# Eight tiles of split matmul input moved to eight different starts in SBUF

## The chip, the cores and the metric

The kernel runs on one core of one Trainium2 chip. The metric is the device time of one execution in microseconds; less is better. Inputs and outputs lie in HBM. SBUF, the on-chip memory that the engines read, has 128 partitions, and a tile takes the same range of bytes in each of them; where this document speaks of the place at which a tile begins, it means the byte within a partition, taken modulo 512.

## What is computed

Linear attention over 4 batches, 8 heads, 576 positions of 64 numbers each, followed by two MLPs over 2304 tokens of width 512 with 2048 hidden units. All is float32. Cut to what matters:

```
proj = x @ w_phi                      # 64 -> 128 features, for q and for k
proj -= max(abs(proj))                # per position
phi(x) = [exp(proj), exp(-proj)]      # 256 features
attn = phi(q) (phi(k)^T v) / (phi(q) sum(phi(k)) + 1e-6)
x = attn, heads side by side          # 2304 x 512
x = leaky_relu(x @ w1_in)  @ w1_out   # 512 -> 2048 -> 512
x = mish(x @ w2_in) @ w2_out
```

## The kernel before, in words

**Exact products out of rounded ones.** TensorE multiplies in the type float32r, which keeps fewer bits than float32. So each float32 operand x is split into a rounded part hi and a rest lo = x - hi, and a product is made of three matmuls into one PSUM bank: weights hi by input hi, weights hi by input lo, weights lo by input hi. `three` (lines 80 to 83) issues them on lines 81, 82 and 83. `split` (lines 76 to 78) makes the two parts: ScalarE rounds a copy into hi (line 77), VectorE subtracts it from the source into lo (line 78). In the names of the profile, a matmul `a<-wl,wh` writes a PSUM tile a, streams the tile wl (the moving operand) and holds 128 columns of wh (the stationary operand, brought in by a weight load, engine PEld, that has the line of its matmul).

**Attention** runs first, pair of heads by pair of heads (32 steps of `attention`, lines 435 to 485). `q_proj` and `k_proj` (lines 316 to 328 and 294 to 302) use `three` with moving operands of 256 or 320 columns; `kv` (line 345) and `nd` (line 373) use plain matmuls of 128 and 65 columns.

**The MLPs.** The tokens are cut into five blocks for each MLP, four of 512 tokens and one of 256, ten blocks in all, and worked through by `moe`. X (line 70) holds the activations transposed, in four chunks (kk = 0 to 3) of 128 features by 2304 tokens. For a block, `window` (lines 492 to 498) splits its four chunks into eight tiles: hi and lo for each kk. `emit_h` (lines 506 to 514) then makes the hidden units, 128 at a time: 16 groups (m), each with four chunks, each with `three`, where the tiles of the window are the moving operand (512 columns, or 256 in the short blocks) and slices of 128 columns of the split weights W are the stationary one. In the trace these are the matmuls `a<-wh,wh`, `a<-wl,wh` and `a<-wh,wl`: a weight tile and a window tile are both called wh or wl there. Window hi is the moving operand on lines 81 and 83, window lo on line 82. After the activation (`leaky`, lines 557 to 573, in the first MLP, `mish`, lines 575 to 622, in the second), whose result is again split into tiles gh and gl, `emit_o` (lines 516 to 533) makes the second product: `b<-gh,wh` and its like in the first MLP, where gh and gl stream, `b<-wh,gh` and its like in the second, where the weights stream.

**What sets the order.** The whole program is scheduled by hand: each engine runs its instructions in the order of the code. `moe` calls `emit_h` of the next groups before `emit_o` of an earlier one. When the last group of a block has been issued, `window` of the next block follows at once (lines 631 to 633). Its tiles are those that the old block's last matmuls still read, so ScalarE's copy for a chunk waits for the last matmul on that chunk, VectorE's subtraction waits for the copy, and TensorE meanwhile runs an `emit_o`.

**Where the tiles lie.** Pools are laid out one after another in the order of lines 62 to 68, slots inside a pool in the order in which their tags are first asked for. The pool of the window, winp (line 63), has four slots for each of its two tags, wh and wl (lines 495 and 496), of 512 numbers of 4 bytes, 2048 bytes each. In the program as built the eight slots begin at byte 53408 and follow each other every 2048 bytes, so all eight begin at 160 modulo 512. X begins at 128 modulo 512. The tiles that come after winp in the MLP stage, gh, gl and the weights W (whose slices of 128 columns are 512 bytes) among them, all begin at 160 modulo 512 too. In the attention stage the split inputs and weights of `q_proj` and `k_proj` begin at 0; `q_proj` streams from column 0 in its first two calls, from column 320 in its third (256 modulo 512) and from column 256 in its fourth (0 again). For `kv` the stationary operand begins at 64 and the moving one at 160 or 416; for `nd` the stationary operand begins at 128 or 384 and the moving one at 128. The last tile of the MLP stage ends at byte 227488 of a partition.

Of the kernel before, what the change touches and what calls it, by code (L numbers as in the profile page):

```python
# [12 lines left out]
F32R = mybir.dt.float32r  # L13
# [11 lines left out]
def attention_two_mlps_kernel(  # L25
# [17 lines left out]
    P = 128  # L43
    KD = DM // P
    M = DFF // P
    MAIN = 512
# [13 lines left out]
    I32 = mybir.dt.int32  # L60

    xp = tc.alloc_tile_pool(name="xp", bufs=1)
    winp = tc.alloc_tile_pool(name="winp", bufs=4)
    gp = tc.alloc_tile_pool(name="gp", bufs=2)
    wp0 = tc.alloc_tile_pool(name="wp0", bufs=1)
    ps = tc.alloc_tile_pool(name="ps", bufs=4, space=PSUM)
# [9 lines left out]
    def split(hi, lo, src):  # L76
        nc.scalar.activation(out=hi, in_=src, func=AF.Copy)
        nc.vector.tensor_tensor(out=lo, in0=src, in1=hi.bitcast(F32), op=ALU.subtract)
# [112 lines left out]
    with tc.manual_schedule():  # L191
# [297 lines left out]
        NB = len(blocks)  # L489
        win = {}  # L490

        def window(j, chunks=range(KD)):
            a, c0, n = blocks[j]
            for kk in chunks:
                hi = winp.tile([P, MAIN], F32R, tag="wh", name="wh")[:, 0:n]
                lo = winp.tile([P, MAIN], F32R, tag="wl", name="wl")[:, 0:n]
                split(hi, lo, X[:, kk, c0:c0 + n])
                win.setdefault(j, []).append((hi, lo))

# [128 lines left out]
        def moe(g):  # L628
            for x in [g, g + 1] if g == jump else [g + 1] if g > jump else [g]:
                if x < len(seq):  # L630
                    emit_h(seq[x])
                    if seq[x][1][-1] == M - 1 and seq[x][0] + 1 < NB:
                        window(seq[x][0] + 1)
# [42 lines left out]
        for n in range(PAIRS + 1):  # L676
            attention(n)
            if 0 <= n - PAIRS // 2 < KD:
                window(0, (n - PAIRS // 2,))
# [43 lines left out]
```

## Time and profile before

| | us |
|---|---|
| median of 3 runs | 1033.09 |
| lowest and highest of them | 1032.63, 1036.21 |
| the profiled execution, its own time | 1029.51 |
| its span in the trace | 1027.7 |

The profile shows that one execution. Engines: PE is TensorE's matmuls, PEld its weight loads (they run beside matmuls), DVE VectorE, ACT ScalarE, POOL GpSimd. A line of a timeline begins with the start and the duration in us. A matmul's duration in the trace includes the way through the array, so successive matmuls overlap in it: what one costs in a full stream is the distance from its start to the start of the next, called the step below. An instruction group in a fence of `--by-form` kind reads: line, engine, operation, out<-in, shapes, count | busy us, mean ns of one | idle time of the engine before them and what ended it.

### The profile page before, as it was taken

To read this page: it belongs to the slowest core of one execution; us is meant where nothing else is said; L and a number is where in the kernel's file an instruction comes from. 1 tells how busy PE (TensorE), PEld (TensorE's weight loads), DVE (VectorE), ACT (ScalarE), POOL (GpSimd) and SP (SyncE) were. 2 spreads that over 40 slices of the span, in tenths; PEclk is the share of its full clock that TensorE was granted. 3 is DMA by queue.
4 is the path that set the end of the run, shared out by engine and by line. 5 is a ranking of instruction groups with operands and counts; after the bars stand their busy time and mean duration, and the time that the engine had idled before them with its cause. 6 is when DMAs were issued, how large, how long until landed. Compare 5 with 4: busy or idle time off the path is not lost.

```text
span 1027.7 us, 14556 instructions
## 1 busy us (share of the span) xinstructions
PE 1001.1 (97%) x5544; PEld 871.2 (85%) x5544; DVE 753.2 (73%) x1389; ACT 501.3 (49%) x839; POOL 72.6 (7%) x38
## 2 busy tenths in 40 slices
PE   6999999999999999999999999999999999999998
PEld 5999988998888888998888888888888988888886
DVE  5888898876995666666533546978876888868976
ACT  4666666654554333343333445545544555545543
POOL 3322333220000000000000000000000000000000
PEclk9999999999999999999999999999999999999999
DMA  4333323313541344444311221000100100001001
GB/s 130 111 111 111 100 82 93 121 43 113 160 148 42 123 144 154 134 144 136 110 62 31 93 82 62 1 1 0 41 1 1 41 1 21 1 1 41 1 1 42
DMA packets 55494, 72.84 MB, mean 71 GB/s; under 512 B 10496, under 2 KB 39808, under 8 KB 55424
## 3 DMA queue, kind: packets, MB, share of 16 engines
q1 hardware_dynamic: 55264, 71.84, 21.6%
q8 instruction: 44, 0.72, 0.3%
q14 instruction: 26, 0.21, 0.1%
q10 hardware_dynamic: 160, 0.07, 0.0%
HBM read 57.48 MB, written 14.42 MB: 70 GB/s over the span
## 4 chain that ended last, share of the span: by engine, by line
PE 92%; DVE 5%; issue 1%; ACT 1%; POOL 0%; ACTq 0%; DVEq 0%; POOLq 0%
PE a L81 14%; PE a L82 14%; PE a L83 14%; PE b L82 13%; PE b L81 13%; PE b L83 13%; PE b L373 6%; PE b L345 4%; DVE qd L335 1%; PE a L266 1%; DVE kd L291 1%; DVE mx L290 1%; ACT kv L353 1%; PE b L395 1%; PE b L350 1%
## 5 line engine op out<-in xcount | busy, mean ns | idle before, releaser
L81 PE MATMUL a<-wh,wh 128*128 128x512 f32 (+1 forms) x640 | 235.6, 368 | 0.0
L82 PE MATMUL a<-wl,wh 128*128 128x512 f32 (+1 forms) x640 | 235.4, 368 | 0.0
L83 PE MATMUL a<-wh,wl 128*128 128x512 f32 (+1 forms) x640 | 235.4, 368 | 0.0
L81 PEld LDWEIGHTS a<-wh,wh 128*128 128x128 f32 x640 | 120.6, 188 | 20.2
L82 PEld LDWEIGHTS a<-wl,wh 128*128 128x128 f32 x640 | 120.7, 189 | 20.1
L83 PEld LDWEIGHTS a<-wh,wl 128*128 128x128 f32 x640 | 120.6, 188 | 20.0
L571 DVE TENSOR_TENSOR gl<-g,gh 128x512 fp32r<-128x512 f32 x72 | 49.9, 693 | 110.1 <-ACT gh L568 110.1
L82 PE MATMUL b<-gl,wh 128*128 128x512 f32 (+1 forms) x320 | 117.7, 368 | 0.0
L81 PE MATMUL b<-gh,wh 128*128 128x512 f32 (+1 forms) x320 | 117.7, 368 | 0.0
L83 PE MATMUL b<-gh,wl 128*128 128x512 f32 (+1 forms) x320 | 117.7, 368 | 0.0
L82 PE MATMUL b<-wl,gh 128*128 128x512 f32 x288 | 112.1, 389 | 0.0
L81 PE MATMUL b<-wh,gh 128*128 128x512 f32 x288 | 112.1, 389 | 0.0
L83 PE MATMUL b<-wh,gl 128*128 128x512 f32 x288 | 112.1, 389 | 0.0
L568 ACT ACTIVATE gh<-g 128x512 fp32r<-128x512 f32 x72 | 45.5, 632 | 115.9 <-PE b L83 109.4
L330 POOL PARTITION_ALL_REDUCE qm<-qd x32 | 71.9, 2249 | 140.7 <-DVE qd L335 122.1
L593 ACT ACTIVATE gh<-u 128x512 fp32r<-128x512 f32 x72 | 45.6, 633 | 70.6 <-PE b L82 63.9
L567 DVE TENSOR_TENSOR g<-g,a 128x512 f32<-128x512 f32 x72 | 49.4, 686 | 38.0 <-ACT g L564 35.2
L150 ACT ACTIVATE c<-c 128x512 f32<-128x512 f32 x64 | 40.3, 630 | 68.5 <-DVE c L147 68.3
L373 PE MATMUL b<-kv,qp 128*128 128x65 f32 x512 | 62.7, 276 | 7.5 <-ACT kv L353 7.5
L620 ACT ACTIVATE r<-e,two 128x512 f32<-128x512 f32 x72 | 51.7, 718 | 36.3 <-DVE e L605 36.3
L83 PEld LDWEIGHTS b<-gh,wl 128*128 128x128 f32 x320 | 60.3, 189 | 10.1
L81 PEld LDWEIGHTS b<-gh,wh 128*128 128x128 f32 x320 | 60.4, 189 | 10.0
(103 smaller groups left out, 1773.7 us busy)
## 6 DMA issues: line engine op xcount, KB each, us to landing
stage<-in_moe_w_in_dram SPq DMA_DIRECT2D x32, 512.0 KB, 3.6
stage<-in_moe_w_out_dram SPq DMA_DIRECT2D x32, 512.0 KB, 3.5
scr<-c SPq DMA_DIRECT2D x37, 256.0 KB, 2.0
wstage<-scr SPq DMA_DIRECT2D x32, 256.0 KB, 3.8
kn<-in_k_dram SPq DMA_DIRECT2D x16, 256.0 KB, 3.8
qn<-in_q_dram SPq DMA_DIRECT2D x16, 256.0 KB, 4.0
vmain<-in_v_dram SPq DMA_DIRECT2D x16, 256.0 KB, 3.2
out_dram<-X SPq DMA_DIRECT2D x16, 256.0 KB, 2.2
```

What stands on the lines that cost most here:

```text
L81: nc.tensor.matmul(out=o, lhsT=wh_, rhs=xh, start=start, stop=False)
L82: nc.tensor.matmul(out=o, lhsT=wh_, rhs=xl, start=False, stop=False)
L83: nc.tensor.matmul(out=o, lhsT=wl_, rhs=xh, start=False, stop=stop)
L150: nc.scalar.activation(out=c, in_=c, func=AF.Copy, scale=2.0 ** -112)
L330: nc.gpsimd.partition_all_reduce(s["qm"][:, h, :], s["qd"][:, h, :], P, bass_isa.ReduceOp.absmax)
L345: nc.tensor.matmul(out=o, lhsT=s["kp"][a][:, h, t, :], rhs=s["vm"][:, h, t:NM + 1:NM - t, :], start=(c == 0 and t == 0), stop=False, skip_ ...
L373: nc.tensor.matmul(out=g[:, 2 * j + h, 0:D + 1], lhsT=s["qp"][a][:, h, Q_COL[h][u]:Q_COL[h][u] + P], rhs=s["kv"][:, 2 * h + a, 0:D + 1], s ...
L567: nc.vector.tensor_tensor(out=g, in0=g, in1=h, op=ALU.max)
L568: nc.scalar.activation(out=hi, in_=g, func=AF.Copy)
L571: nc.vector.tensor_tensor(out=lo, in0=g, in1=hi.bitcast(F32), op=ALU.subtract)
L593: nc.scalar.activation(out=hi2, in_=u2, func=AF.Copy)
L620: nc.scalar.activation(out=r0, in_=e0, func=AF.Ln, bias=two)
```

## The change

The pool winp gets one slot per tag instead of four, and eight tags instead of two, one for each pair of part (h or l) and chunk (0 to 3). Each slot is 528 numbers long instead of 512, 2112 bytes instead of 2048, and the tile is a slice of it that begins o numbers into the slot, where o is 0 for chunks 0 and 1, 0 (hi) and 4 (lo) for chunk 2, and 2 (hi) and 12 (lo) for chunk 3. No instruction is added or removed.

```diff
-    winp = tc.alloc_tile_pool(name="winp", bufs=4)
+    winp = tc.alloc_tile_pool(name="winp", bufs=1)
...
+        STEP = 16
+        PLACE = ((0, 0), (0, 0), (0, 4), (2, 12))
+
         def window(j, chunks=range(KD)):
+
+
             a, c0, n = blocks[j]
             for kk in chunks:
-                hi = winp.tile([P, MAIN], F32R, tag="wh", name="wh")[:, 0:n]
-                lo = winp.tile([P, MAIN], F32R, tag="wl", name="wl")[:, 0:n]
+                hi, lo = (winp.tile([P, MAIN + STEP], F32R, tag=f"w{x}{kk}", name=f"w{x}")[:, o:o + n]
+                          for x, o in zip("hl", PLACE[kk]))
                 split(hi, lo, X[:, kk, c0:c0 + n])
                 win.setdefault(j, []).append((hi, lo))
```

## Rows read from the trace of the kernel before

**Rows 1.** The page: busy time of each engine, and the granted clock in 40 slices
```profile
PE 1001.1 (97%) x5544; PEld 871.2 (85%) x5544; DVE 753.2 (73%) x1389; ACT 501.3 (49%) x839; POOL 72.6 (7%) x38
...
PEclk9999999999999999999999999999999999999999
```

**Rows 2.** Busy time by stretch: attention, change of stage, MLPs
```profile
core 0: us, PE busy (x) PEld busy (x) DVE busy (x) ACT busy (x) POOL busy (x), PEclk, DMA share, GB/s
0.00:220.00 220.00, 198.56 (x1672) 193.47 (x1673) 182.52 (x405) 138.91 (x238) 70.87 (x38) 1.00 0.34 104
250.00:440.00 190.00, 190.00 (x959) 162.56 (x958) 135.41 (x244) 78.79 (x137) 0.00 (x0) 1.00 0.40 130
640.00:1027.00 387.00, 383.15 (x1780) 320.62 (x1778) 310.84 (x523) 192.16 (x308) 0.00 (x0) 1.00 0.04 13
```

**Rows 3.** The page: the chain that ended last, by engine
```profile
PE 92%; DVE 5%; issue 1%; ACT 1%; POOL 0%; ACTq 0%; DVEq 0%; POOLq 0%
```

**Rows 4.** Groups of matmuls by line and shape that stream a tile of the window
```profile
L81 PE MATMUL a<-wh,wh 128*128 128x512 f32 x512 | 199.5, 390 | 0.0
L82 PE MATMUL a<-wl,wh 128*128 128x512 f32 x512 | 199.2, 389 | 0.0
L83 PE MATMUL a<-wh,wl 128*128 128x512 f32 x512 | 199.2, 389 | 0.0
...
L83 PE MATMUL a<-wh,wl 128*128 128x256 f32 x128 | 36.2, 283 | 0.0
```

**Rows 5.** Timeline of PE in the first MLP: start us, duration us
```profile
400.28 0.39 PE L82 MATMUL a<-wl,wh 128*128 128x512 f32 x1
...
400.96 0.39 PE L82 MATMUL a<-wl,wh 128*128 128x512 f32 x1
401.18 0.39 PE L83 MATMUL a<-wh,wl 128*128 128x512 f32 x1
401.41 0.39 PE L81 MATMUL b<-gh,wh 128*128 128x512 f32 x1
401.64 0.39 PE L82 MATMUL b<-gl,wh 128*128 128x512 f32 x1
```

**Rows 6.** Timeline of PEld in the same stretch
```profile
400.28 0.19 PEld L83 LDWEIGHTS a<-wh,wl 128*128 128x128 f32 x1
400.51 0.19 PEld L81 LDWEIGHTS a<-wh,wh 128*128 128x128 f32 x1
```

**Rows 7.** Timeline of PE where the first short block begins
```profile
415.37 0.28 PE L81 MATMUL a<-wh,wh 128*128 128x256 f32 x1
415.48 0.28 PE L82 MATMUL a<-wl,wh 128*128 128x256 f32 x1
415.60 0.28 PE L83 MATMUL a<-wh,wl 128*128 128x256 f32 x1
415.72 0.28 PE L81 MATMUL a<-wh,wh 128*128 128x256 f32 x1
```

**Rows 8.** Timeline of PE in attention: the third and fourth call of q_proj, k_proj between
```profile
46.18 0.28 PE L82 MATMUL a<-qtl,wbh 128*128 128x256 f32 x1
46.30 0.29 PE L83 MATMUL a<-qth,wbl 128*128 128x256 f32 x1
46.43 0.28 PE L81 MATMUL a<-wbh,kth 128*128 128x256 f32 x1
46.55 0.28 PE L82 MATMUL a<-wbl,kth 128*128 128x256 f32 x1
...
47.29 0.31 PE L82 MATMUL a<-qtl,wbh 128*128 128x320 f32 x1
47.44 0.31 PE L83 MATMUL a<-qth,wbl 128*128 128x320 f32 x1
47.59 2.84 PE L345 MATMUL b<-vmain,kp 128*128 128x128 f32 x24
```

**Rows 9.** Timeline of PE in attention: matmuls of nd
```profile
41.37 1.39 PE L373 MATMUL b<-kv,qp 128*128 128x65 f32 x11
```

**Rows 10.** Groups of ScalarE and VectorE: the split of the window, the split in leaky
```profile
L571 DVE TENSOR_TENSOR gl<-g,gh 128x512 fp32r<-128x512 f32 x72 | 49.9, 693 | 110.1 <-ACT gh L568 110.1
...
L78 DVE TENSOR_TENSOR wl<-X,wh 128x512 fp32r<-128x512 f32 x32 | 21.0, 689 | 13.4 <-ACT wh L77 13.3
...
L77 ACT ACTIVATE wh<-X 128x512 fp32r<-128x512 f32 x32 | 19.0, 629 | 14.2 <-PE a L83 13.7
```

**Rows 11.** Timeline where a block ends: its successor's split, and the first matmul on it
```profile
701.47 2.68 ACT L77 ACTIVATE wh<-X 128x512 fp32r<-128x512 f32 x4 [4.43 <-PE a L83]
702.13 2.74 DVE L78 TENSOR_TENSOR wl<-X,wh 128x512 fp32r<-128x512 f32 x4 [4.33 <-ACT wh L77]
...
706.03 0.39 PE L81 MATMUL a<-wh,wh 128*128 128x512 f32 x1
```

## The prediction

> **What bounds the kernel now.** I read the busy times first: TensorE's matmuls fill 97% of the span, and the granted clock is full in every slice, which is the upper of its two levels, 2.4 GHz [rows 1]. By stretch, attention leaves TensorE gaps, but the MLPs, which are what the change touches, leave none: 190.00 of 190.00 us in the first, 383.15 of 387.00 in the second [rows 2]. The chain that ended last is TensorE for 92% [rows 3]. So whatever the change does to the time it must do to the step from one matmul to the next. Work saved or added on ScalarE or VectorE counts only if TensorE comes to wait for it.
>
> Which matmuls? Those that stream a window tile are three groups of 512 with 512 columns and, on the same three lines, three of 128 with 256 columns: 1536 + 384 = 1920, with no idle time before any [rows 4]. Their step is the quantity to cost. In a full stream of 512 columns it is (401.64 - 400.28) / 6 = 0.2267 us [rows 5]. At 2.4 GHz and one column per cycle 512 columns take 0.2133, so 13.3 ns of each step are something else. Those 13.3 ns are all that another place could give back, and the rest of this text is about whether they depend on the place.
>
> **The change, part by part.**
>
> *Instructions, waits, queues.* None is added, removed or moved. Before, four slots per tag were used in turn by four chunks per block, so chunk kk always had slot kk and waited for the same chunk of the block before; with a tag for each chunk it waits for the same. No DMA touches these tiles. Term: 0.
>
> *Where the rest goes.* Eight slots grow by 64 bytes each, 512 in all, so every tile behind winp moves by 512 bytes and keeps its place modulo 512; the last ends at 228000. Term: 0, and X lies ahead of winp.
>
> *The new places.* From 160, in steps of 64 with the offsets 16, 8 and 48 bytes added, in the order hi0, lo0, hi1, ...: 160, 224, 288, 352, 416, 496, 40, 144. Modulo 64 the first five stay at 32, as before; lo2, hi3 and lo3 come to 48, 40 and 16. The slots are whole multiples of 64 bytes, so I see no rounding by which the tiles would not come to these places.
>
> *The split.* ScalarE writes hi in 629 ns, VectorE writes lo in 689 [rows 10]; there are 40 of each, 32 of them of 512 columns. VectorE's 689 read X at 128 and hi at 160; the subtraction of leaky reads both inputs at 160 and takes 693 [rows 10], so 32 bytes of difference between inputs is worth 4 ns at most. Where a block ends, the four subtractions are done at 702.13 + 2.74 = 704.87, and TensorE streams the first chunk at 706.03 [rows 11]: 1.16 us of cover, that of the last chunk longer by the nine matmuls ahead of it. The three copies and subtractions on shifted tiles would have to become slower by over 1.16 us together before TensorE waited. If that cover were gone, each further 100 ns on one of them would cost at most 100 ns at each of nine block boundaries, 0.9 us. Term: 0.
>
> *512-column steps, eight places modulo 512.* Is 13.3 ns a price of the common place? Today the next weight load starts with the matmul, within 0.01 us [rows 5, 6], and both read from 160. The trace has other pairs. q_proj's third call streams from 256 against weights at 0 and steps 0.12 and 0.13 us; k_proj right after, both operands at 0, steps 0.12 [rows 8]; the short blocks, both at 160, step 0.12 [rows 7]. So three distances and absolute places make one figure at 256 columns. Matmuls of 320 columns at place 0 step 0.15, (47.59 - 47.29) / 2, against 0.133 of columns [rows 8]: a surplus of about 12 to 17 ns with starts printed to 0.01 us, as at 160. For kv (distance 96 or 352 bytes) 24 starts span 2.84 - 0.28 = 2.56 us, or 0.111 each [rows 8]; for nd (distance 0 or 256) 11 starts span 1.39 - 0.28 = 1.11, again 0.111 [rows 9] (0.28 us being the duration of such a short matmul). Here, too, the distance changes nothing. The reason may be that a load moves 512 bytes while the stream moves about twice that, so they pass each other modulo 512 whatever the starts. What no row shows is two matmuls in a row whose moving operands begin at different places, except at the seam of q_proj and k_proj just quoted (0.13 against 0.12). Bounds: a gain of all 13.3 ns on 1536, 20.4 us; a loss of the same size, since a figure of 13 ns is the only disturbance of a step that the rows show, 20.4 us. I take 0, by the 256-column rows, which are nearest.
>
> Here a rule bears on the step. The Trainium skill (TensorE: Matmul & The Clock Gate, "Wait — 56ns, not 53.3ns?") gives 215.7 ns for 512 columns in bf16. By that figure 11 ns of each of the 1536 steps are not inherent, 16.9 us, but the row here has 226.7 for window tiles and for gh and gl alike, and no run here shows 215.7 for this type.
>
> *256-column steps.* A short block's first step is 0.11, all later ones 0.12 [rows 7]. If places alone set that, 0.01 x 384 = 3.8 us could be gained, or lost. I take 0, since the first follows 512-column matmuls, during which its successor's weights had time, and so differs in more than place.
>
> *Starts inside 64 bytes.* Of the 12 matmuls per group of hidden units, hi3 feeds two (lines 81 and 83), lo2 and lo3 one each (line 82): a third, 512 + 128 = 640. Below: 0, as the step at 160 (32 bytes inside 64) is that at 0 [rows 7, 8]. A gain lies within the 20.4 us above. Above: if a stream that doesn't begin on 16 or 32 bytes ran at half rate, 512 x 213 ns + 128 x 107 ns = 123 us. In between, one more 13.3 ns per matmul: 8.5 us. I take 0 by the nearest row, keep 8.5 for the range, and the 123 for a tail.
>
> **Sum.** 0. Against the profiled execution, 1029.51 us with a span of 1027.7, that is 1029.5; that execution was 3.6 us below the median of the runs, so I state it against the median: 1033.0, with +-5 us for the case's own range, 1028 to 1038. A difference of 0.5%, 5.2 us, is about what a measurement of this kernel can tell from no change.
>
> **The rivals.**
>
> *The common place costs something (faster).* If the streams' starts at the same place collide, with the weights or with the stream just ended, and different starts part them, the steps shrink. For it: the 13.3 ns are there in every 512-column step, and every operand in the MLPs begins at 160. Against it: the pairs of kv and nd, of q_proj and k_proj, whose distances differ and whose steps don't [rows 8, 9]. All of it on all tiles: 20.4 + 3.8 = 24.2 us, 1009; on the third of the matmuls that begin elsewhere inside 64 bytes, 8.1 us, 1025. It decides above 5.2 us / 1920 = 2.7 ns per matmul. Chance 0.20, most of it for the partial forms.
>
> *A start inside a line costs more reads (slower).* Place: the 640 matmuls on lo2, hi3 and lo3. Price: one more 13.3 ns each gives 8.5 us, 1041.6; half rate gives 1156. It passes 0.5% from 8.1 ns per matmul on. For it: starts at 8, 16 or 48 bytes beside a multiple of 32 do not occur in TensorE's streams here, so no row excludes it. Against it: 32 bytes inside 64 costs nothing visible, and a shifted stream of 2048 bytes still is one unbroken run. Chance 0.14, of which 0.03 for half rate.
>
> The Trainium skill (SBUF — State Buffer, Specifications) speaks of lines of 16 bytes, where each cross to a new line has a price. By that only hi3, 8 bytes into such a line, crosses one line more in 128; 1/128 of 0.2267 us on its 320 matmuls is 0.6 us, an estimate that stays within the forecast's own range, but it does name the tile on which this rival would show first. No row here shows it.
>
> *No change.* Chance 0.66.
>
> **How the numbers follow.** The likeliest case gives 1033.0. Its own range, 1028 to 1038, holds 0.65. Down to 1024 the range takes in the third-of-the-matmuls form of the faster case (0.07), up to 1042 the one-more-price form of the slower one (0.08): 0.80 in all. Left out are the full gain, 1009, and half rate.
>
> **What would show it.** Right: the 512-column step of the window's matmuls stays 0.2267 in each of the twelve positions of a group, the 256-column step 0.12, L77 and L78 keep 629 and 689 ns, PE stays busy throughout 250 to 440. The faster case: steps between 0.213 and 0.224 on `a<-wh,wh` while `b<-gh,wh` keeps 0.2267. The slower one: every fourth or so step longer, at chunks 2 (line 82) and 3. The forecast is wrong if the three lines of the window's matmuls show different steps by chunk, and the sum over 1920 exceeds 5 us.

## The result, and the profile after

The kernel became slower: 1043.98 us, median of 6 runs (1042.34 to 1047.44), against 1032.86 us for 6 runs of the kernel before. The ratio is 1.0109, with a 95% interval from 1.0083 to 1.0135, so 8.6 to 13.9 us more. The forecast, 1033.0 with a range of 1024 to 1042, missed it, and "slower" had been given a chance of 0.14.

The profiled execution took 1044.73 us, with a span of 1042.9. Two lines of its page:

```profile
PE 1016.7 (97%) x5544; PEld 873.4 (84%) x5544; DVE 753.3 (72%) x1389; ACT 500.9 (48%) x839; POOL 72.6 (7%) x38
...
PEclk9999999899999999999999999999999999999999
```

TensorE is busier by 15.6 us, with the same 5544 matmuls; VectorE and ScalarE have what they had [rows 1]. So the time is in TensorE's steps and not in a wait. The split of the window has kept its price too, 689 ns for the subtraction [rows 10] (groups by form, as there):

```profile
L78 DVE TENSOR_TENSOR wl<-X,wh 128x512 fp32r<-128x512 f32 x32 | 21.1, 689 | 13.4 <-ACT wh L77 13.2
```

The groups of matmuls by form show where the time went. The end of a matmul is modelled in the trace, so its duration only points at the place; the steps further down, from start to start, decide. The last line is the same group as the one above it, in the trace of the kernel before:

```profile
L83 PE MATMUL a<-wh,wl 128*128 128x512 f32 x512 | 203.3, 397 | 0.0
L82 PE MATMUL a<-wl,wh 128*128 128x512 f32 x512 | 201.5, 394 | 0.0
L81 PE MATMUL a<-wh,wh 128*128 128x512 f32 x512 | 200.8, 392 | 0.0
...
L83 PE MATMUL b<-gh,wl 128*128 128x512 f32 x256 | 100.8, 394 | 0.0
```

```profile
L83 PE MATMUL b<-gh,wl 128*128 128x512 f32 x256 | 99.6, 389 | 0.0
```

The three lines of the window's matmuls went from 389 or 390 to 392 (line 81), 394 (line 82) and 397 ns (line 83) [rows 4]. The fourth line is a surprise: `b<-gh,wl` belongs to `emit_o`, whose operands the change left at one place, and it is at 394 where it was at 389 before, with a step of 0.2267 us [rows 5].

One group of hidden units and the `emit_o` behind it, in the first MLP (timeline of PE: start, duration):

```profile
387.84 0.39 PE L81 MATMUL a<-wh,wh 128*128 128x512 f32 x1
388.06 0.40 PE L82 MATMUL a<-wl,wh 128*128 128x512 f32 x1
388.30 0.40 PE L83 MATMUL a<-wh,wl 128*128 128x512 f32 x1
388.54 0.39 PE L81 MATMUL a<-wh,wh 128*128 128x512 f32 x1
...
390.63 0.39 PE L81 MATMUL b<-gh,wh 128*128 128x512 f32 x1
...
391.09 0.40 PE L83 MATMUL b<-gh,wl 128*128 128x512 f32 x1
391.33 0.39 PE L81 MATMUL b<-gh,wh 128*128 128x512 f32 x1
391.55 0.39 PE L82 MATMUL b<-gl,wh 128*128 128x512 f32 x1
...
392.71 0.39 PE L81 MATMUL b<-gh,wh 128*128 128x512 f32 x1
...
393.39 0.39 PE L81 MATMUL a<-wh,wh 128*128 128x512 f32 x1
```

Twelve steps of the window take 390.63 - 387.84 = 2.79 us, 232.5 ns each, where they took 226.7. They are uneven: 0.22, 0.24, 0.24 for the first three. The twelve of `emit_o` take 2.76 us, 230.0 each, again uneven (0.24 and then 0.22 from 391.09 on), until the last three, at (393.39 - 392.71) / 3 = 0.227, are back at the old step. So a disturbance that begins in the window's matmuls outlives them by nine matmuls.

The trace of before holds such a case already. Here is the first window group of 512 columns behind a short block, all operands at 160, and the matmul behind the group:

```profile
449.92 0.40 PE L81 MATMUL a<-wh,wh 128*128 128x512 f32 x1
...
452.67 0.28 PE L81 MATMUL b<-gh,wh 128*128 128x256 f32 x1
```

Its twelve steps take 2.75 us, 229.2 ns each instead of 226.7, though no operand lies elsewhere: a 512-column step depends on the matmuls ahead of it, too.

The short blocks went the other way. Here is a group of 24 matmuls of 256 columns in the second MLP, its first and the first matmul behind it:

```profile
844.06 0.28 PE L81 MATMUL a<-wh,wh 128*128 128x256 f32 x1
...
846.87 0.39 PE L81 MATMUL b<-wh,gh 128*128 128x512 f32 x1
```

2.81 us / 24 = 117 ns, where 120 stood before [rows 7].

Together: 1536 window steps of 512 columns x (232.5 - 226.7) = +8.9 us; 1536 steps of 512 columns in `emit_o` behind them x (230.0 - 226.7) = +5.1 us; 384 short steps x -2.5 ns or so = -1.0 us. That is +13 us, at the upper end of the interval. (The means over all groups of the trace, 232.6 and 229.6 ns for the 512-column steps, give 12.7.) A run of the changed kernel at a mean granted clock of 1.000 took 1042.34 us and the profiled one before, at 0.999, 1029.51, a difference of 12.8 us. The two profiled executions differ by 15.2 us; some 2 us of that are in attention, where this execution was granted a lower clock (a stretch with the columns of [rows 2]), 0.94 in the mean where every slice before was full [rows 1]:

```profile
160.00:220.00 60.00, 56.19 (x455) 55.01 (x454) 49.88 (x109) 37.29 (x65) 18.85 (x9) 0.94 0.28 88
```

### The profile page after: what moved, and what is told of

It reads as the page before. It is cut to its first block, busy times and chain, and to the rows that moved or that the text cites. A ratio compares the mean times of both kernels' runs of the same rounds, so it can differ in the third digit from the quotient of the medians.

```text
span 1042.9 us, 14556 instructions
## 1 busy us (share of the span) xinstructions
PE 1016.7 (97%) x5544; PEld 873.4 (84%) x5544; DVE 753.3 (72%) x1389; ACT 500.9 (48%) x839; POOL 72.6 (7%) x38
## 4 chain that ended last, share of the span: by engine, by line
PE 92%; DVE 5%; issue 1%; ACT 1%; POOL 0%; ACTq 0%; DVEq 0%; POOLq 0%
PE a L83 14%; PE a L81 14%; PE a L82 14%; PE b L82 13%; PE b L83 13%; PE b L81 13%; PE b L373 6%; PE b L345 4%; DVE qd L335 1%; PE a L266 1%; DVE mx L290 1%; DVE kd L291 1%; ACT kv L353 1%; PE b L395 1%; PE b L350 1%
## 5 line engine op out<-in xcount | busy, mean ns | idle before, releaser
L83 PE MATMUL a<-wh,wl 128*128 128x512 f32 (+1 forms) x640 | 239.2, 374 | 0.0
L82 PEld LDWEIGHTS b<-gl,wh 128*128 128x128 f32 x320 | 60.3, 188 | 11.6
L373 PEld LDWEIGHTS b<-kv,qp 128*128 128x128 f32 x512 | 61.4, 196 | 10.3 <-ACT kv L353 10.0
```

The lines of the kernel that those rows point to most:

```text
L82: nc.tensor.matmul(out=o, lhsT=wh_, rhs=xl, start=False, stop=False)
L83: nc.tensor.matmul(out=o, lhsT=wl_, rhs=xh, start=False, stop=stop)
L373: nc.tensor.matmul(out=g[:, 2 * j + h, 0:D + 1], lhsT=s["qp"][a][:, h, Q_COL[h][u]:Q_COL[h][u] + P], rhs=s["kv"][:, 2 * h + a, 0:D + 1], s ...
```

## The experiments

Three theories stood at the start. Theory 1, succession: a step grows when a stream begins at another place than the one before. Theory 2: the three starts inside 64 bytes cost. Theory 3: what counts is the distance between the place where a stream begins and that of the weights that are loaded beside it. Times stand against runs of the kernel before on the same chip. Where a fence shows two rows, they are the first matmul of a group of twelve window matmuls and the first of `emit_o` behind it, so the difference of their starts is twelve steps.

### a_places: the eight places without the offsets

```diff
-        PLACE = ((0, 0), (0, 0), (0, 4), (2, 12))
+        PLACE = ((0, 0), (0, 0), (0, 0), (0, 0))
```

> The eight places in steps of 64 bytes are kept, the three offsets inside 64 bytes are set to 0. Theory 1 (succession: a 512-column step grows when a stream begins at another place than the stream before it): nearly all of the loss stays, 8 to 12 us over the kernel before. Theory 2 (the starts inside 64 bytes cost): the time falls back to that of the kernel before, within 3 us. Theory 3 (the distance between the place of a stream and that of the weights loaded beside it): most of the loss stays, 6 us or more.

Measured: 1044.45 us against 1029.92, ratio 1.0138 (1.0118 to 1.0157). The timeline, with the end of `emit_o` as a third row:

```profile
386.21 0.39 PE L81 MATMUL a<-wh,wh 128*128 128x512 f32 x1
...
389.00 0.40 PE L81 MATMUL b<-gh,wh 128*128 128x512 f32 x1
...
391.77 0.39 PE L81 MATMUL a<-wh,wh 128*128 128x512 f32 x1
```

2.79 us for the window, as with the offsets, and 2.77 us for `emit_o`. The whole loss stays without any new offset inside 64 bytes; as the cause of this result theory 2 falls.

### b_inside: the offsets without the eight places

```diff
+        AT = {(0, 0): 0, (0, 1): 512, (1, 0): 1024, (1, 1): 1536, (2, 0): 2048,
+              (3, 0): 2560 + 2, (2, 1): 3072 + 4, (3, 1): 3584 + 12}
+        WIN = winp.tile([P, 8 * MAIN + 128], F32R, name="win")
...
+                hi, lo = (WIN[:, AT[kk, x]:AT[kk, x] + n] for x in range(2))
```

> All eight tiles lie at one place modulo 512, but for the offsets of 8, 16 and 48 bytes of the same three tiles. Theory 1: the starts still differ, by less than 64 bytes and in the second half of each group only, so a loss of 0 to 4 us. Theory 2: the whole loss, 9 us or more. Theory 3: 0 to 3 us.

Measured: 1037.87 against 1029.92 us, ratio 1.0068 (1.0046 to 1.0089), so about 7 us.

```profile
387.94 0.39 PE L81 MATMUL a<-win,wh 128*128 128x512 f32 x1
...
390.69 0.40 PE L81 MATMUL b<-gh,wh 128*128 128x512 f32 x1
```

2.75 us, 229.2 ns per step. No theory had this: 8, 16 and 48 bytes on a third of the matmuls cost about half of what the eight places cost (7 us of 14; 2.5 ns per window step of 5.8), while on top of the eight places they added nothing (2.79 us both times). The two parts of the change are not a sum.

### c_common: all eight tiles together, another place for each block

```diff
+        HI = (0, 16, 16, 32, 48, 64, 80, 80, 96, 112)
+        LO = (0, 16, 16, 32, 48, 64, 80, 80, 96, 112)
+        WIN = winp.tile([P, 8 * MAIN + 128], F32R, name="win")
...
+                hi = WIN[:, kk * MAIN + HI[j]:kk * MAIN + HI[j] + n]
+                lo = WIN[:, (KD + kk) * MAIN + LO[j]:(KD + kk) * MAIN + LO[j] + n]
```

> All eight tiles of a block at one place, but another one for each block: 0, 64, 128, 192, 256, 320, 384, 448 bytes beyond 160 in the eight blocks of 512 tokens. Theory 1: the 512-column steps inside a group are 0.2267 us in every block, since neighbours begin at the same place. Theory 2: 0.2267 too. Theory 3: the step differs from block to block, by 3 ns or more.

Measured: 1040.6 us (one run) against 1029.92. One group each of the blocks at 64, 192 and 256 bytes:

```profile
386.37 0.40 PE L81 MATMUL a<-win,wh 128*128 128x512 f32 x1
...
389.13 0.40 PE L81 MATMUL b<-gh,wh 128*128 128x512 f32 x1
...
609.13 0.39 PE L81 MATMUL a<-win,wh 128*128 128x512 f32 x1
...
611.93 0.39 PE L81 MATMUL b<-gh,wh 128*128 128x512 f32 x1
...
685.69 0.39 PE L81 MATMUL a<-win,wh 128*128 128x512 f32 x1
...
688.41 0.39 PE L81 MATMUL b<-wh,gh 128*128 128x512 f32 x1
```

230.0 ns at 64, 233.3 at 192, 226.7 at 256. In every block all neighbours begin at one place, and still the steps differ: theory 1 falls as the whole explanation. The block at 256 equals that at 0, and the blocks at 320, 384 and 448 repeat those at 64, 128 and 192 (means over the block: 230.3, 232.6 and 233.3 ns against 230.3, 232.7 and 233.3), so places count modulo 256, not modulo 512.

### d_lo: hi left in place, lo moved

```diff
+        HI = (0, 0, 0, 0, 0, 0, 0, 0, 0, 0)
+        LO = (0, 16, 16, 32, 48, 64, 80, 80, 96, 112)
```

(The rest is as in c_common.)

> The four hi tiles stay at 160; the four lo tiles begin 0, 64, 128, 192, 256, 320, 384, 448 bytes further in the eight blocks of 512 tokens. Theory 1: 0.2267 us in the first block and 3 to 14 ns more on lines 82 and 83 in the others. Theory 2: 0.2267 everywhere. Theory 3: longer or shorter on the steps of line 82 alone, 0.2267 on lines 81 and 83.

Measured: 1036.06 us (one run) against 1029.92. The start of a group in the block whose lo lies 64 bytes further, lines 81 and 83 and then 81 of the next chunk, and the end of the group:

```profile
384.23 0.39 PE L81 MATMUL a<-win,wh 128*128 128x512 f32 x1
...
384.69 0.40 PE L83 MATMUL a<-win,wl 128*128 128x512 f32 x1
384.93 0.39 PE L81 MATMUL a<-win,wh 128*128 128x512 f32 x1
...
387.00 0.40 PE L81 MATMUL b<-gh,wh 128*128 128x512 f32 x1
```

230.8 ns with a third of the streams moved by 64; with 256 (682.34 to 685.06) it is 226.7. Theory 3 had put the cost on line 82 alone; 12 x 4.1 = 49 ns on four matmuls would be 12 ns each, but the matmul of line 83 at 384.69, whose stream stayed in place, steps by 0.24, too. That can be the carry-over seen in `emit_o`. Theory 1 had named lines 82 and 83, so this run alone does not part the two.

### e_fine and f_fine: places by the byte

```diff
-        HI = (0, 16, 16, 32, 48, 64, 80, 80, 96, 112)
+        HI = (2, 4, 4, 6, 8, 10, 12, 12, 14, 24)
```

(LO the same; f_fine has 28, 36, 36, 40, 44, 52, 56, 56, 60, 62.)

> All eight tiles of a block at one place, 8, 16, 24, 32, 40, 48, 56 and 96 bytes beyond the place of the weights in the eight blocks of 512 tokens. Theory 3a (the distance to the weights decides, by the byte): steps differ already at 8 to 56 bytes, between 0.2267 and 0.2335 us. Theory 3b (only whole lines of 64 bytes decide): 0.2267 up to 56, then that of 64 (0.229) at 96.

> The same with 112, 144, 160, 176, 208, 224, 240 and 248 bytes. The distance counted modulo 256 (as 0 and 256, 64 and 320 agreed) means that the steps come back towards 0.2267 us as 248 nears 256, if the distance decides by the byte; if whole lines decide, 208 to 248 all have the 0.2333 of 192. A place with a step under 0.2267 would be a gain, which no theory so far names.

Measured: 1044.53 and 1044.23 us (one run each) against 1032.94. From e_fine the blocks at 8 and 96 bytes, then from f_fine that at 248:

```profile
298.90 0.40 PE L81 MATMUL a<-win,wh 128*128 128x512 f32 x1
...
301.69 0.40 PE L81 MATMUL b<-gh,wh 128*128 128x512 f32 x1
...
999.18 0.40 PE L81 MATMUL a<-win,wh 128*128 128x512 f32 x1
...
1001.99 0.40 PE L81 MATMUL b<-wh,gh 128*128 128x512 f32 x1
```

```profile
999.04 0.40 PE L81 MATMUL a<-win,wh 128*128 128x512 f32 x1
...
1001.84 0.39 PE L81 MATMUL b<-wh,gh 128*128 128x512 f32 x1
```

232.5 ns at 8 bytes, 234.2 at 96, 233.3 at 248, which is 8 bytes short of 256. Theory 3b (whole lines) falls; of 3a the expectation that steps come back as 256 nears falls as well. Only the same place modulo 256 gives 226.7; everywhere else that was tried, from 8 bytes on, the mean over a block lies between 230.3 and 234.6 ns, and no place is below 226.7.

### g_all64: everything moved together

```diff
     X = xp.tile([P, KD, NT], F32, name="X")
+    winp.tile([P, 16], F32, tag="pad", name="pad", bufs=1)
```

> The kernel before with 64 bytes left out ahead of the window's pool, so that the window, gh, gl and all weights move together by 64 bytes. Theory 3 (distance to the weights): steps stay 0.2267 us in the MLPs, time as before within 2 us. Rival (the absolute place modulo 256 decides): the steps of 64 bytes of c_common, 0.229 on average, in the window's matmuls and in emit_o too, 7 to 9 us more.

Measured: 1036.2 us (one run) against 1032.94. In the timeline (lines are one higher in this kernel), and in the stretch of attention that the windows show:

```profile
389.06 0.39 PE L82 MATMUL a<-wh,wh 128*128 128x512 f32 x1
...
391.78 0.39 PE L82 MATMUL b<-gh,wh 128*128 128x512 f32 x1
```

```profile
160.00:220.00 60.00, 57.16 (x424) 56.09 (x423) 46.60 (x100) 35.78 (x60) 17.93 (x8) 0.86 0.28 88
```

226.7 ns with window and weights both at 224: moved together, they keep the old step, so it is not the absolute place that costs. The 3.3 us are not in the MLPs' steps; the stretch of attention had a mean clock of 0.86, and fewer matmuls ran in it, 424 against 476 in the profiled execution of the kernel before, whose clock there was full.

### h_weights: the window left in place, half of the weights moved

```diff
+            if (which, m) == (0, 8):
+                wp.tile([P, 16], F32R, tag="pad", name="pad")
             W[which, m] = [pool.tile([P, 2, KD, P], F32R, tag=f"{t}{m}", name=f"w{t}{m}") for t in "hl"]
```

> The kernel before with its window at 160; the weights of hidden groups 8 to 15 lie 64 bytes further, at 224. Theory 3 (distance of the stream to the weights loaded beside it, modulo 256): groups 0 to 7 keep 0.2267 us; in groups 8 to 15 the window streams 64 bytes behind the weights, which is 192 modulo 256, so 0.2333 us; in emit_o of the first MLP the same 0.2333, in the second MLP, where the weights stream and gh is loaded, 0.229. About 1536 / 2 x 6.7 + 384 x 6.7 + 432 x 2.3 ns = 5.1 + 2.6 + 1.0 = 8 to 9 us in all, short blocks aside. Rival (only where the window itself lies matters): all steps 0.2267.

Measured: 1040.25 us (one run) against 1030.28, 10.0 more where 8 to 9 were expected. Groups 6 and 12 (counted from 0) of one block of the first MLP, then the place where group 8 of another block follows an `emit_o`:

```profile
573.96 0.39 PE L81 MATMUL a<-wh,wh 128*128 128x512 f32 x1
...
576.68 0.39 PE L81 MATMUL b<-gh,wh 128*128 128x512 f32 x1
...
607.13 0.40 PE L81 MATMUL a<-wh,wh 128*128 128x512 f32 x1
...
609.93 0.40 PE L81 MATMUL b<-gh,wh 128*128 128x512 f32 x1
```

```profile
362.10 0.39 PE L83 MATMUL b<-gh,wl 128*128 128x512 f32 x1
362.32 0.40 PE L81 MATMUL a<-wh,wh 128*128 128x512 f32 x1
362.56 0.39 PE L82 MATMUL a<-wl,wh 128*128 128x512 f32 x1
```

226.7 ns with weights at 160, 233.3 with weights at 224, as was worked out from c_common's block at 192 bytes. The window was not touched here. This is the run that shows the main part of theory 3: the distance from the weights, with its sign (192 and not 64), decides, whichever of the two is moved. It does not show the words "loaded beside it". The trace has the first moved weights loaded beside the matmul at 362.10, whose step stays at 0.22; the next one, the first that uses moved weights, is the first to step by 0.24, and so it is at group 8 of every long block. In the runs that moved the window all weights lie at one place, so they can't tell a matmul's own weights from those of the next.

### i_load: half a weight load

```diff
-                    three(hb[it][:, i * n:(i + 1) * n], hi[:, 0, kk, :], lo[:, 0, kk, :], win[j][kk][0], win[j][kk][1],
-                          start=(kk == 0), stop=(kk == KD - 1))
+                    o, (xh, xl) = hb[it][:, i * n:(i + 1) * n], win[j][kk]
+                    half = slice(0, P if kk in (0, KD - 1) else P // 2)
...
+                    nc.tensor.matmul(out=o[half], lhsT=lo[:, 0, kk, half], rhs=xh, start=False, stop=(kk == KD - 1))
```

> The kernel before; in chunks 1 and 2 the third matmul of each product (line 83 before) loads and uses only 64 of its 128 weight columns, so half of that correction is left out for those chunks. Theory L (the 13.3 ns over the columns of a 512-column step come from the weights that are loaded beside the stream, in proportion to their bytes): the step of the second matmul in chunks 1 and 2, beside which the short load runs, falls by some 7 ns to 0.220 us, 256 steps, about 1.7 us in all, if the steps after it do not lose it again. Rival (the 13.3 ns belong to each stream's own start): all steps 0.2267.

Measured: 1033.7 us (one run) against 1030.28. The second and third matmul of chunk 1 and the first of chunk 2 (lines 516, 517 and 515 of this kernel), then the end of the group:

```profile
384.77 0.39 PE L516 MATMUL a<-wl,wh 128*128 128x512 f32 x1
384.99 0.40 PE L517 MATMUL a<-wh,wl 128*64 128x512 f32 x1
385.23 0.39 PE L515 MATMUL a<-wh,wh 128*128 128x512 f32 x1
...
386.61 0.40 PE L81 MATMUL b<-gh,wh 128*128 128x512 f32 x1
```

The twelve steps, from 383.86 on, became longer, 2.75 us. The matmul beside the short load (at 384.77) kept about 0.22 to 0.23, and the one after it, which uses the 64 columns, rose to 0.24. So neither side was right: the 13.3 ns do not shrink with the load, and a load of another length, with a matmul that uses half the weight columns, disturbs the steps like another place does. What the 13.3 ns of the undisturbed step are stays open.

### j_short: can the faster short steps be kept?

```diff
+        HI = (0, 0, 36, 0, 0, 0, 0, 36, 0, 0)
```

(LO the same.)

> Only the two short blocks' tiles are shifted, by 144 bytes, all eight together; the other blocks stay at 160. By the rows of f_fine the 384 steps of 256 columns fall from 0.120 to 0.118 us, 0.8 us less, and the 512-column steps of emit_o behind short groups in the second MLP may give 0.2 us more: 0 to 1 us less than the kernel before, within 0.2% of it, and too little to tell by its time.

Measured: 1030.89 us against 1030.28, with a ratio of 0.9989 (0.9974 to 1.0005). A short group of the second MLP:

```profile
837.10 0.28 PE L81 MATMUL a<-win,wh 128*128 128x256 f32 x1
...
839.90 0.39 PE L81 MATMUL b<-wh,gh 128*128 128x512 f32 x1
```

116.7 ns per short step where 120 stood, so the gain is there in the trace; in the time it can't be told from none.

## Why the prediction was wrong

**The bound was read rightly.** No wait, no split and no queue changed anything, and the whole loss is in the step of TensorE's matmuls, as the first part said it would have to be.

**The step that failed is "512-column steps, eight places modulo 512", priced at 0** because "three distances and absolute places make one figure". They were one distance. q_proj's third call lies 256 bytes from its weights, its neighbours 0 [rows 8], and c_common shows, for 512 columns, that 256 and 0 are the same. kv's two distances, 96 and 352, also differ by 256, as do nd's 0 and 256. That left kv against nd [rows 8, 9] as the only unlike pair, and its 0.111 us says nothing: its streams of 65 and 128 columns, 27 and 53 ns, are far shorter than the step. The short blocks show how such a figure misleads: with 256 columns an unlike distance makes a step not longer but 2 to 3 ns shorter. The rows for a 512-column stream at an unlike distance did not exist in the trace of before; it had been worked out that the loss could be 20.4 us, and that bound was then given no rival. The term priced at 0 measured 8.9 us.

**"... they pass each other modulo 512 whatever the starts"** was the reason offered for the 0; e_fine refutes it, as 8 bytes already cost 5.8 ns. Nor do the rows give "about twice that": in the 0.19 us of a load [rows 6] a stream of 2048 bytes per 0.2267 us moves some 1.7 KB, over three times the load's 512 bytes. The Trainium skill (TensorE: Matmul & The Clock Gate, "Step-by-step: what each phase is for") says that "Loading the next tile's weights doesn't steal SBUF read bandwidth from the running matmul". For this type and shape the place of the weights does change the running step: with weights moved by 64 bytes and the stream left alone, it went from 226.7 to 233.3 ns. Whether it is the load of the next weights that does it, the runs don't show: where only that load was a moved one (h_weights at 362.10), the step stayed.

**A term was missing for `emit_o`.** The sum counts the 1920 window matmuls alone, and the sign of the faster case has "`b<-gh,wh` keeps 0.2267": the price of a step was taken to belong to its own operands. It carries over to the next nine matmuls, which added 5.1 us, over a third of the loss. The trace of before could have warned of it, by the 229.2 ns behind a short block.

**The slower rival had the wrong place.** It put the price on the 640 matmuls that start inside 64 bytes. a_places gives those no offset and loses as much. Its amount, 8.5 us and 1041.6, came near by chance. Starts inside 64 bytes do cost when nothing else differs (b_inside, 7 us), but as one more unlike distance: in c_common multiples of 64 cost as much. Lines of 16 bytes do not part them either: the blocks of e_fine at 16, 32 and 48 bytes, whole lines all, average 231.5, 233.6 and 233.4 ns per step, beside 233.1 at 8.

**The faster rival** fell: no place gave a 512-column step below 226.7. Its short-block term had the right sign in part, -1.0 of at most -3.8 us.

Shown, for float32r matmuls of 512 columns: where all streams of a group lie at one distance from the weights, that distance, modulo 256 bytes, sets the step, and 0 is the best of those tried. Not shown: which load counts, and by what mechanism inside the chip. Nor are the prices of single distances enough for the change itself, which mixes them. By the block means of c_common (226.7, 230.3, 232.7 and 233.3 ns at 0, 64, 128 and 192) the groups of a_places would average 230.4, and they took 232.5; those of d_lo at 64 would average 227.9, and they took 231.3. So going from one distance to another costs something besides. Whether that is carry-over or a price of succession stays open.

## What to carry to other kernels

Where float32r matmuls of 512 columns fill TensorE, let moving and stationary operands begin at the same place modulo 256 bytes; pools laid out in powers of two gave this unasked here, and a pad between the two that is no multiple of 256 takes it away: here 6 ns per matmul on the moved tiles, and 3 on each of those behind them. Before a price of 0 is read from rows that "differ", check modulo what they differ, and whether the quantity in question is what limits them.

## What was not expected of the hardware

A group at one common unlike distance settles into a repeating pattern (at 192 bytes 233.3 ns per step; at 64 some 229, after a few longer steps), and back at distance 0 it takes some matmuls to return to 226.7: nine in the changed kernel, from two to ten in nearly all groups of the other runs. Steps shorter than the settled one occur on the way, such as 0.22 at 391.33 to 391.55. With 256 columns an unlike distance shortens the step, from 120 to 117 ns. And with 512 columns the step becomes longer where only half of the weights are loaded and used.
